# Query projections as whole matmuls up to pair 32, weight loads on SyncE, and two-pair cycles

## The chip, the cores and the metric

The kernel runs on one core of one Trainium2 chip. The metric is device time in microseconds of one execution. TensorE (PE) multiplies into PSUM, VectorE (DVE) and ScalarE (ACT) read PSUM and work on SBUF, GpSimd (POOL) works on SBUF alone, and DMAs are issued from the queues of SyncE (SP), ScalarE and GpSimd. Each engine runs its own instructions in order and waits on semaphores for the others. A transfer that waits at the head of an engine's queue holds up whatever that engine would issue behind it.

## The reference

One transformer block on 2048 tokens of width 512, in float32: attention with 32 query heads of 16 that share one key and one value head, then a gated FFN of inner width 1792.

```python
q = (x @ wq).reshape(B, S, 32, 16)           # per head
k = x @ wk                                   # one head of 16
v = x @ wv
scores = einsum("bhqd,bkd->bhqk", q, k) * 16 ** -0.5
o = einsum("bhqk,bkd->bhqd", softmax(scores), v)
h = A_x + o.reshape(B, S, 512) @ wo          # x above is layernorm(A_x)
y = layernorm(h)
out = h + (gelu(y @ w_gate) * (y @ w_up)) @ w_down
```

Matrix operands are split into a high and a low part, both of type float32r, and a product is the sum of three terms: high by high, high by low, low by high.

## The kernel before

**Tiling.** The 2048 tokens are four blocks of 512 (`NB`, `T`). The 32 heads are eight groups of four (`NG`). Keys come in 16 chunks of 128 (`KC`). A block's attention is thus 8 x 16 key steps, and each key step has two *pairs* of heads. `score(n)` (L1014) issues pair n: two score matmuls into one PSUM tile `s`, one exp on ScalarE (L404) into half of a tile `p`. When a key step's two pairs are done, `weigh` (L406) multiplies `p` by the values into the accumulator `acc`; `finish(k)` (L991) issues the k oldest weighings that are pending. A group is 32 pairs, a block 256.

**Row halves.** A score has a contraction of 50 rows (`KR`): three products of 16 and two rows for a bound that is subtracted before the exp. Keys and queries lie twice in SBUF, at rows 0 and 64. The two score matmuls of a pair take the two row halves of TensorE's array. Where a step of other work is set *beside* a score, the score moves to the one half and the other half takes a matmul with 64 rows of contraction.

**Query projection.** `project_q(b, cs, ...)` (L187) projects block b's queries in four chunks of 128 columns (eight heads). A chunk has 12 terms. As *whole* matmuls with 128 rows they are issued alone, three to a `yield`; as *halves* each term is issued twice, once per half of the rows (lane 0, then lane 1), each beside a score. Between a whole and a half phase, and between lane 0 and lane 1, VectorE copies one column of the bank (`mark`, L211). A finished chunk is split into `qh` and `ql` (two buffers each) and stored to the DRAM tensor `q_d` by three SyncE transfers (L242). For the chunks in `HURRY` VectorE or ScalarE first copies the bank to `raw`, which frees the bank; there is one bank for projections at this point (`width = 1`). After the four chunks the norm of the queries is taken (`pqn`, L255) and the bound row is stored (`bound`, L280) some cycles later, when `age()` says so.

**Order.** Block 0's first chunk is projected in the prologue (`q_first`), and the rest of it (`q_rest`) nearly so: at pair 0 there remain the split of its chunk 3 and its norm. `later_q` (L305) makes the rest: chunk 0 of block 1 whole, chunk 1 half whole and half in halves (`FULL_STEPS`, `BREAK`), all others in halves. `RAMP` gives two steps of it ahead of pairs 3, 5 and 7. From pair 8 to pair 272 (`lead`) the main loop (L1058) runs *cycles* of three pairs: up to four half steps beside the second and third pair, then up to two weighings of key steps that are done, then perhaps one step of weight preparation. Lane 0 takes four halves a cycle; lane 1 takes four or two, by what the cycle before it weighed.

**Weight preparation.** `part_weights` (L495) has 46 steps: it loads 256 KB of wo, w_gate, w_up or w_down, POOL splits it into high and low (and halves w_down), and 512 KB are written to DRAM tensors for the dense part. POOL issues both the load (L503), one step ahead, and the store. Two of three cycles take a step.

**SyncE and VectorE.** Both run an order written out by hand (L1044): what the program issues first stands first in their queues. On SyncE these are the `q_d` stores, `load_q` (L375, issued with the fifth pair of a group for the next group, so 28 pairs ahead), and in block 0 for each finished group the write of the evicted accumulator `oT` to `acc_d` (L425) and its read-back in four transfers to `oc` (L434), which VectorE inverts, multiplies and splits into `o_hi` and `o_lo`.

**End of block 0.** At pair 256 the queries' memory is given back after `check_bound` (L1439), and POOL issues two 1 MB loads of wo. When pair 260 is next, `dense(0)` (L623) is started: two loads of x and four of w1 on SyncE. From pair 272 on the output projection of block 0 (`pp`, L596) runs beside the scores of block 1; its first terms need `o_hi` of chunks 0 to 2, its later ones chunk 3, which is made of groups 6 and 7. The FFN (`pg`, `pu`, `pd`) follows.

Of the kernel before, what the change touches and what calls it, by code (L numbers as in the profile page):

```python
# [9 lines left out]
F32 = mybir.dt.float32  # L10
# [9 lines left out]
P = 128  # L20
# [6 lines left out]
PB = 5  # L27
# [2 lines left out]

W2 = 3

LAG = 6

FIRST_Q = 1

FULL_STEPS = 18

HURRY = ((0, 3), (1, 0))

BREAK = (1, 1)

RAMP = {3: 2, 5: 2, 7: 2}

# [4 lines left out]
CUT, EDGE, GAP, HOLD, REST = -1, -2, -3, -4, -5  # L49
# [3 lines left out]
def kernel(  # L53
# [12 lines left out]
    nc = tc.nc  # L66
# [91 lines left out]
    def run(outer, first):  # L158
# [27 lines left out]

        def project_q(b, cs, eng, col, whole=None):  # L187
            halves = whole is not None
            whole = whole if halves else {c: 3 * DC for c in cs}
            tsl = slice(b * T, (b + 1) * T)  # L190
            xT_hi, xT_lo = xT[b]
            urgent = b == 0 and cs[0] == 0
# [1 line left out]
            for c in cs:  # L194
                pq = psum1(f"pq_{b}_{c}")
                terms = [
                    (wt[:, d, c * P : (c + 1) * P], xt[:, d, :])
                    for d in range(DC)
                    for wt, xt in ((wq_hi, xT_hi), (wq_hi, xT_lo), (wq_lo, xT_hi))
                ]  # L200
                last = len(terms) - 1
                full = whole.get(c, 0)
                for n, (lhsT, rhs) in enumerate(terms[:full]):
                    nc.tensor.matmul(
                        pq, lhsT, rhs, start=(n == 0), stop=(n == last), skip_group_check=full <= last
                    )
                    if n % 3 == 2 and (urgent or n < last):
                        yield 3
                for a in range(2) if full <= last else ():
                    if a or full:  # L210
                        mark = eb.tile([P, 1], F32, tag="qmark", bufs=2, name=f"mark_{b}_{c}_{a}")  # L211
                        nc.vector.tensor_copy(mark, pq[:, :1])
                    rows = slice(64 * a, 64 * a + 64)
                    for n, (lhsT, rhs) in list(enumerate(terms))[full:]:
                        yield a, last - n, partial(
                            nc.tensor.matmul, pq, lhsT[rows], rhs[rows],
                            start=(a == 0 and n == 0), stop=(a == 1 and n == last),
                            skip_group_check=True,
                        )

                raw = None
                if (b, c) in HURRY:
                    raw = eb.tile([P, T], F32, tag="vT", bufs=3, name=f"pq_raw_{b}_{c}")
                    if b == 0:
                        nc.scalar.activation(raw, pq, AF.Copy)
                    else:
                        nc.vector.tensor_copy(raw, pq)
                    yield 3
                qh = eb.tile([P, T], F32R, tag="qh", bufs=2, name=f"qh_{b}_{c}")
                ql = eb.tile([P, T], F32R, tag="ql", bufs=2, name=f"ql_{b}_{c}")  # L230
                if raw is not None:
                    split(nc.vector, qh, ql, raw)
                else:

                    split(nc.vector if b == 0 and c == FIRST_Q else eng, qh, ql, pq)
                qs = eb.tile([P, T], BF16, tag="qs", bufs=DC, name=f"qs_{b}_{c}")
                (nc.gpsimd if urgent else nc.vector).tensor_tensor(
                    qs, qh.bitcast(F32), qh.bitcast(F32), op=ALU.mult
                )
                qss.append(qs)  # L240
                for r0, part in ((0, qh), (DH, ql), (2 * DH, qh)):
                    nc.sync.dma_start(  # L242
                        q_d[c * HC : (c + 1) * HC, r0 : r0 + DH, tsl].bitcast(F32),
                        part.bitcast(F32),
                    )
                if not halves and (raw is None or b == 0):
                    yield 3
                if (b, c) == BREAK:
                    yield HOLD

            if halves:
                yield REST
# [51 lines left out]

        def later_q():  # L305

            second = project_q(1, range(DC), nc.vector, 1, {0: 3 * DC, 1: FULL_STEPS - 3 * DC})
            for _ in range(sum(RAMP.values())):
                yield next(second)

            next(q_rest)
            for token in second:
                if token == HOLD:
                    yield REST
                    for _ in q_rest:
                        pass
                else:
                    yield token
            for b in range(2, NB):
                yield from project_q(b, range(DC), nc.vector, b, {})  # L320

        def age():
            for entry in after:
# [16 lines left out]
        def first_bound(qg):  # L340

            m = ms[0]
            for u in range(2):
                for a, eng in enumerate((nc.sync, nc.scalar)):
                    eng.dma_start(
                        qg[64 * a + 3 * DH : 64 * a + 3 * DH + 1, 2 * u + a, :].bitcast(F32),
                        m[2 * u + a : 2 * u + a + 1, :].bitcast(F32),
                    )
            hs = slice(0, FIRST_Q * HC)
            nc.sync.dma_start(q_d[hs, 3 * DH, :T].bitcast(F32), m[hs].bitcast(F32))  # L350
            for a in range(2):
                nc.sync.dma_start(
                    qg[64 * a : 64 * a + KR, 1 - a :: 2, :].bitcast(F32),
                    q_d.rearrange("h r s -> r h s")[:, 1 - a : 4 : 2, :T].bitcast(F32),
                )

        def advance(gen, n):
            while n > 0:
# [136 lines left out]
        def part_weights(pw):  # L495
# [3 lines left out]


            def load_f(src, name):
                raw = pw.tile([P, D], F32, tag="w_raw", bufs=2, name=f"{name}r")
                nc.gpsimd.dma_start(raw.rearrange("p (c n) -> p c n", n=src.shape[-1]), src)  # L503
                return raw

            def part_f(name, halve, raw):
# [22 lines left out]
            for f in range(FC):  # L529
# [9 lines left out]
                    partial(load_f, wd_t[:, f : f + 1, :], name),  # L539
                    partial(part_f, name, True), partial(store_2, w2_d[f]),  # L540
                ))
            raws, left = {0: steps[0][0]()}, None
            for i, (_, part, store) in enumerate(steps):
                if left is not None:
                    left()
                if i + 1 < len(steps):
                    raws[i + 1] = steps[i + 1][0]()
                both = part(raws.pop(i))
                left = partial(store, both)
                yield 1  # L550
# [440 lines left out]
        def finish(n):  # L991
            for _ in range(min(n, len(pend))):
                pb, pg, pkc, pp, pacc, _ = pend.pop(0)
                weigh(pacc, pp, pkc)
                if pkc == KC - 1:
                    evacuate(pb, pg, pacc)
# [45 lines left out]
        LEAD = (3, 2, 2)  # L1042
        n, lead = 0, 2 * PER + sum(SIZES[: LEAD[0]])
        with tc.manual_schedule(engines={mybir.EngineType.SP, mybir.EngineType.DVE}):  # L1044
            parts, said = None, 3
            if first:
                work = later_q()
                parts = part_weights(early.enter_context(tc.tile_pool(name="parts", bufs=1)))

            while n < 2 * PB - 2:  # L1050
                for _ in range(RAMP.get(n, 0) if first else 0):
                    next(work)
                score(n)
                n += 1
            finish(len(pend) - 2)

            token, ran = next(work) if first else None, 2
            for cycle in range((lead - n) // 3):  # L1058
                age()
                rest = token == REST  # L1060
                count = 0
                if token is not None and not rest:
                    count = min(4 if ran < 2 or token[0] == 0 else 2, token[1] + 1)
                for j in range(3):
                    if n == 2 * PER:
                        assert token is None
                        while after:
                            age()
                        for _ in parts or ():
                            pass  # L1070
                        if first:
                            check_bound(eb, k2m)
                        parts = work = None
                        early.close()
                        db = late.enter_context(tc.tile_pool(name="dense", bufs=1))
                        load_wo(0)
                    if 0 < j <= count // 2:
# [15 lines left out]
                finish(ran)  # L1093
                if outs:
                    take_out()
                if parts is not None and cycle > 2 and cycle % 3 < 2:
                    next(parts, None)
            assert n == lead
        assert not outs
# [421 lines left out]
```

## Time and profile before

| | |
|---|---|
| Time, median of 3 runs | 1446.84 us (1445.14 to 1448.3) |
| Profiled execution, time | 1445.67 us |
| Profiled execution, span | 1444.0 us |
| TensorE busy | 1406.6 us (97%) |
| ScalarE busy | 1041.9 us (72%) |
| VectorE busy | 542.3 us (38%) |
| GpSimd busy | 231.3 us (16%) |
| Mean granted TensorE clock | 0.992 |
| Exps (L404) | 1024, 1029 ns each |
| Moved by DMA | 194.09 MB, 134 GB/s on average |

The span runs from the first to the last instruction, and the device time has a little around it. A busy TensorE isn't TensorE at its peak: matmuls are pipelined, and each shows as busy from its start to its modelled end, so overlapping ones hide how closely they follow one another. A row of the timeline gives the start, the time that it covers, the engine and the line, what is written from what, and how many instructions were merged; in brackets stands the idle time ahead of it and what ended that.

### The profile page before, as it was taken

Reading aid. Unit: us, or ns where it says so; the run is one execution under the profiler, and the core shown is the slowest. Engines: PE = TensorE matmul, PEld = TensorE weight load, DVE = VectorE, ACT = ScalarE, POOL = GpSimd, SP = SyncE. Lnnn points to the kernel's source line nnn. Section 1 sums busy time; section 2 is a strip of 40 time slices with the busy share of each in tenths; the row PEclk is TensorE's granted clock in tenths of the full one; section 3 lists DMA queues with packets and bytes.
Section 4 is the critical chain, followed back from the end, with each engine's and each line's share of the span. In section 5 each row is a group of like instructions: output and inputs, shape, how many; then the busy total and the mean of one; then the engine's idle time right before and its main releaser. Section 6 shows DMA issues by size and latency. Waiting matters only on the chain.

```text
span 1444.0 us, 25562 instructions
## 1 busy us (share of the span) xinstructions
PE 1406.6 (97%) x10628; PEld 789.6 (55%) x10628; DVE 542.3 (38%) x975; ACT 1041.9 (72%) x1149; POOL 231.3 (16%) x332
## 2 busy tenths in 40 slices
PE   9799999997999999999999999999999999999998
PEld 7433333333555555555555555555565555557886
DVE  7411313211344332423344242423344242426665
ACT  7489999996777777787777777777777787773000
POOL 6447677650100000000000000000000000002000
PEclk9899999998999999999999999999999999999999
DMA  4556776754144141305144231324144231435551
GB/s 156 157 172 235 240 234 219 222 183 158 41 172 143 41 146 53 132 27 202 51 149 143 70 135 36 132 85 143 56 143 143 83 124 36 144 125 202 176 203 63
DMA packets 71224, 194.09 MB, mean 134 GB/s; under 512 B 9696, under 2 KB 9696, under 8 KB 71068
## 3 DMA queue, kind: packets, MB, share of 16 engines
q1 hardware_dynamic: 60052, 154.00, 31.5%
q0 software_dynamic: 10880, 38.28, 8.0%
q8 instruction: 85, 1.39, 0.4%
q14 instruction: 39, 0.32, 0.1%
q10 hardware_dynamic: 168, 0.10, 0.0%
HBM read 142.53 MB, written 49.55 MB: 133 GB/s over the span
## 4 chain that ended last, share of the span: by engine, by line
PE 86%; ACT 6%; DMA 3%; DVE 2%; issue 1%; SPq 1%; POOL 0%; ACTq 0%; DVEq 0%; POOLq 0%
PE acc L408 30%; PE s L400 18%; PE pu L919 10%; PE pg L919 7%; ACT p L404 6%; PE pd L919 4%; PE pd L596 3%; PE pd L618 3%; PE pg L618 3%; PE pu L618 3%; PE pq L398 2%; PE pp L596 2%; DMA acc_d<-oT 1%; PE pp L727 1%; DMA q_d<-qh 1%
## 5 line engine op out<-in xcount | busy, mean ns | idle before, releaser
L404 ACT ACTIVATE p<-s 128x1024 f32<-128x1024 f32 x1024 | 970.5, 1029 | 259.6 <-PE s L400 257.8
L408 PE MATMUL acc<-p,v_sb 128*32 128x512 f32 x4096 | 493.6, 601 | 0.2 <-DVE oT L421 0.2
L400 PE MATMUL s<-qg,kaug 50*128 50x512 f32 x1984 | 422.1, 427 | 8.9 <-ACT p L404 8.7
L400 PEld LDWEIGHTS s<-qg,kaug 50*128 50x128 f32 x1984 | 191.0, 184 | 259.4 <-ACT p L404 131.4
L408 PEld LDWEIGHTS acc<-p,v_sb 128*32 128x32 f32 x4096 | 112.5, 109 | 237.8 <-issue 233.4
L919 PE MATMUL pu<-x2h,w 64*128 64x512 f32 x672 | 211.5, 391 | 0.0
L919 PE MATMUL pg<-x2h,w 64*128 64x512 f32 x672 | 211.0, 390 | 0.0
L919 PEld LDWEIGHTS pu<-x2h,w 64*128 64x128 f32 x672 | 115.8, 185 | 16.8
L919 PEld LDWEIGHTS pg<-x2h,w 64*128 64x128 f32 x672 | 116.0, 185 | 11.5 <-DVE h L861 0.2
L919 PE MATMUL pg<-x2l,w 64*128 64x512 f32 x336 | 121.9, 390 | 0.0
L919 PE MATMUL pu<-x2l,w 64*128 64x512 f32 x336 | 121.8, 390 | 0.0
L129 POOL TENSOR_SCALAR rstd<-mv 128x1 f32<-128x1 f32 x16 | 3.5, 222 | 683.9 <-DVE mv L127 683.8
L796 ACT ACTIVATE ga<-ga 128x512 f32<-128x512 f32 x56 | 35.3, 634 | 89.2 <-DVE ga L791 89.2
L919 PE MATMUL pd<-w,gh 64*128 64x512 f32 x384 | 81.2, 392 | 0.0
L861 DVE TENSOR_TENSOR h<-h,pd 128x512 f32<-128x512 f32 x48 | 31.9, 684 | 115.5 <-PE pd L919 66.4
L448 DVE RECIPROCAL oc<-oc 128x128 f32<-128x128 f32 x64 | 56.4, 921 | 38.2 <-DMA oc<-acc_d 33.5
L1148 DVE SCALAR_TENSOR_TENSOR ga<-ga,g 128x512 f32<-128x512 f32 x70 | 48.3, 691 | 52.2 <-ACT ga L796 51.1
L919 PEld LDWEIGHTS pu<-x2l,w 64*128 64x128 f32 x336 | 57.9, 185 | 8.1
L780 DVE COPY g<-pg 128x512 f32<-128x512 f32 x56 | 38.7, 692 | 62.5 <-PE pg L919 56.8
L919 PEld LDWEIGHTS pg<-x2l,w 64*128 64x128 f32 x336 | 58.0, 185 | 6.0
L421 DVE COPY oT<-acc 128x512 f32<-128x512 f32 x32 | 22.1, 691 | 89.3 <-PE acc L408 89.1
L793 DVE TENSOR_TENSOR g<-g,pu 128x512 f32<-128x512 f32 x56 | 38.2, 682 | 40.2 <-PE pu L919 30.3
(277 smaller groups left out, 1487.3 us busy)
## 6 DMA issues: line engine op xcount, KB each, us to landing
w<-w_d SPq DMA_DIRECT2D x112, 512.0 KB
w<-w_d SPq DMA_DIRECT2D x28, 1024.0 KB
qg<-q_d SPq DMA_DIRECT2D x48, 200.0 KB
q_d<-qh SPq DMA_DIRECT2D x32, 256.0 KB
acc_d<-oT SPq DMA_DIRECT2D x31, 256.0 KB
oc<-acc_d SPq DMA_DIRECT2D x124, 64.0 KB
w_d<-w_0b POOLq DMA_DIRECT2D x14, 512.0 KB, 5.0
w_d<-w_1b POOLq DMA_DIRECT2D x14, 512.0 KB, 5.7
```

Of the source, the lines that this page charges most:

```text
L400: nc.tensor.matmul(s[:, a, :], kaug[rows, kc * P : (kc + 1) * P], qg[rows, 2 * u + a, :], start=True, stop=True,)
L404: nc.scalar.activation(p[:, 2 * u : 2 * u + 2, :], s, AF.Exp, scale=SCALE)
L408: nc.tensor.matmul(acc[32 * j : 32 * j + 32, :], v_sb[:, kc, :], p[:, j, :], start=(kc == 0), stop=(kc == KC - 1), skip_group_check=True,)
L448: nc.vector.reciprocal(oc[:, 1, sl], oc[:, 1, sl])
L596: nc.tensor.matmul(banks[k], lhsT[rows], rhs[rows], start=(turn == 0 and i == 0), stop=(turn == 1 and i == n - 1), skip_group_check=True,)
L618: nc.tensor.matmul(bank, lhsT, rhs, start=(i == 0), stop=(i == len(ts) - 1))
L780: nc.vector.tensor_copy(g, pg)
L793: nc.vector.tensor_tensor(g, g, pu, op=ALU.mult)
L796: nc.scalar.activation(a, a, AF.Tanh, scale=GELU_A * GELU_C)
L861: nc.vector.tensor_tensor(hs[t], hs[t], pd, op=ALU.add)
L919: nc.tensor.matmul(e["bank"], lhsT[rows], rhs[rows], start=i == 0 and not e["both"], stop=last and e["both"], skip_group_check=True,)
L1148: (soon or lazy).pop(0)()
```

## The change

`RAMP` stays, but up to pair 32 (`2 * KC`) there are only whole matmuls: chunks 0 and 1 of block 1 are both whole, and chunk 1 joins `HURRY`, so its bank is copied out at once. After the ramp one step of `later_q` is taken ahead of every fourth pair (11, 15, 19, ...) until it yields 0, which it does behind block 0's norm. Every fourth pair, all but two pending weighings are issued, and at pairs 16, 20, 28 and 32 one step of weight preparation. `first_bound` no longer loads the second copy of group 0's queries, which only pairs with a step beside them need.

From pair 32 on the cycles run as before, with three differences. After every third finished chunk, lane 1 of the next one takes four halves in each cycle. Weight preparation is stepped by the pair number (`n % 9 != 8`). And once projection has ended, a cycle that begins at an even pair has two pairs in place of three.

The weight loads are issued on SyncE, three steps ahead, into four buffers in place of two. POOL keeps the splits and the stores.

```diff
+AHEAD_W = 3
-FULL_STEPS = 18
-HURRY = ((0, 3), (1, 0))
-BREAK = (1, 1)
+HURRY = ((0, 3), (1, 0), (1, 1))
...
-                for a in range(2) if full <= last else ():
-                    if a or full:
+                for a in range(2) if not full else ():
+                    if a:
...
-            second = project_q(1, range(DC), nc.vector, 1, {0: 3 * DC, 1: FULL_STEPS - 3 * DC})
+            second = project_q(1, range(DC), nc.vector, 1, (0, 1))
             for _ in range(sum(RAMP.values())):
                 yield next(second)
             next(q_rest)
-            for token in second:
-                if token == HOLD:
-                    yield REST
-                    for _ in q_rest:
-                        pass
-                else:
-                    yield token
+            for _ in range(2 * DC - sum(RAMP.values())):
+                yield next(second)
+            yield from q_rest
+            yield 0
+            yield from second
...
             hs = slice(0, FIRST_Q * HC)
             nc.sync.dma_start(q_d[hs, 3 * DH, :T].bitcast(F32), m[hs].bitcast(F32))
-            for a in range(2):
-                nc.sync.dma_start(
-                    qg[64 * a : 64 * a + KR, 1 - a :: 2, :].bitcast(F32),
-                    q_d.rearrange("h r s -> r h s")[:, 1 - a : 4 : 2, :T].bitcast(F32),
-                )
...
-                raw = pw.tile([P, D], F32, tag="w_raw", bufs=2, name=f"{name}r")
-                nc.gpsimd.dma_start(raw.rearrange("p (c n) -> p c n", n=src.shape[-1]), src)
+                raw = pw.tile([P, D], F32, tag="w_raw", bufs=AHEAD_W + 1, name=f"{name}r")
+                nc.sync.dma_start(raw.rearrange("p (c n) -> p c n", n=src.shape[-1]), src)
...
-            raws, left = {0: steps[0][0]()}, None
+            raws, left = {i: steps[i][0]() for i in range(AHEAD_W)}, None
             for i, (_, part, store) in enumerate(steps):
                 if left is not None:
                     left()
-                if i + 1 < len(steps):
-                    raws[i + 1] = steps[i + 1][0]()
+                if i + AHEAD_W < len(steps):
+                    raws[i + AHEAD_W] = steps[i + AHEAD_W][0]()
...
-            parts, said = None, 3
+            parts, said = None, 3 if first else 0
...
-            while n < 2 * PB - 2:
-                for _ in range(RAMP.get(n, 0) if first else 0):
-                    next(work)
+            while n < 2 * KC:
+                for _ in range(RAMP.get(n, n > 7 and n % 4 == 3) if said else 0):
+                    said = next(work)
+                    age()
                 score(n)
                 n += 1
-            finish(len(pend) - 2)
+                if n % 4 == 0:
+                    finish(len(pend) - 2)
+                    if parts is not None and n > 12 and n % 24:
+                        next(parts)
-            token, ran = next(work) if first else None, 2
-            for cycle in range((lead - n) // 3):
+            token, ran, done = next(work) if first else None, 2, 0
+            while n < lead:
...
-                    count = min(4 if ran < 2 or token[0] == 0 else 2, token[1] + 1)
-                for j in range(3):
+                    count = min(4 if ran < 2 or token[0] == 0 or done % 3 == 0 else 2, token[1] + 1)
+                    done += token[0] == 1 and token[1] + 1 == count
+                for j in range(2 if token is None and n % 2 == 0 else 3):
...
-                if parts is not None and cycle > 2 and cycle % 3 < 2:
+                if parts is not None and n % 9 != 8:
                     next(parts, None)
```

More of the change, by code (lines that the diff above doesn't have):

```diff
@@ L188, in project_q @@
             halves = whole is not None
-            whole = whole if halves else {c: 3 * DC for c in cs}
+            whole = whole if halves else cs
             tsl = slice(b * T, (b + 1) * T)
@@ L201, in project_q @@
                 last = len(terms) - 1
[L202 to L205, printed above, removed]
-                    )
+                full = c in whole
+                for n, (lhsT, rhs) in enumerate(terms if full else ()):
+                    nc.tensor.matmul(pq, lhsT, rhs, start=(n == 0), stop=(n == last))
                     if n % 3 == 2 and (urgent or n < last):
                         yield 3
-                for a in range(2) if full <= last else ():
-                    if a or full:
-                        mark = eb.tile([P, 1], F32, tag="qmark", bufs=2, name=f"mark_{b}_{c}_{a}")
+                for a in range(2) if not full else ():
+                    if a:
+                        mark = eb.tile([P, 1], F32, tag="qmark", bufs=2, name=f"mark_{b}_{c}")
                         nc.vector.tensor_copy(mark, pq[:, :1])
                     rows = slice(64 * a, 64 * a + 64)
-                    for n, (lhsT, rhs) in list(enumerate(terms))[full:]:
+                    for n, (lhsT, rhs) in enumerate(terms):
                         yield a, last - n, partial(
@@ L247, in project_q @@
                     yield 3
-                if (b, c) == BREAK:
-                    yield HOLD
             if halves:
@@ L311, in later_q @@
             next(q_rest)
-            for token in second:
-                if token == HOLD:
-                    yield REST
-                    for _ in q_rest:
-                        pass
-                else:
-                    yield token
+            for _ in range(2 * DC - sum(RAMP.values())):
[3 more added lines that the diff above has]
+            yield from second
             for b in range(2, NB):
-                yield from project_q(b, range(DC), nc.vector, b, {})
+                yield from project_q(b, range(DC), nc.vector, b, ())
         def age():
@@ L350, in first_bound @@
             nc.sync.dma_start(q_d[hs, 3 * DH, :T].bitcast(F32), m[hs].bitcast(F32))
-            for a in range(2):
-                nc.sync.dma_start(
-                    qg[64 * a : 64 * a + KR, 1 - a :: 2, :].bitcast(F32),
-                    q_d.rearrange("h r s -> r h s")[:, 1 - a : 4 : 2, :T].bitcast(F32),
-                )
         def advance(gen, n):
```

## The prediction

> **What bounds the kernel now.** I read the 40 slices first, for where an engine falls away, then ScalarE's instructions in order of time, then what stood ahead of each gap, and last the same stretch of a later block for comparison.
>
> ```profile
> span 1444.0 us, 25562 instructions
> ...
> ACT  7489999996777777787777777777777787773000
> ```
>
> ScalarE is at 9 from slice 4 on, which is the attention of block 0 with the query projections beside it; from slice 10 the FFN shares TensorE and ScalarE is no bound. The change touches slices 1 to 10, so I went through the exps there. One exp (L404) is one pair.
>
> ```profile
> 61.28 1.02 ACT L404 ACTIVATE p<-s 128x1024 f32<-128x1024 f32 x1 [1.29 <-PE s L400]
> 70.66 1.94 ACT L404 ACTIVATE p<-s 128x1024 f32<-128x1024 f32 x2 [8.36 <-PE s L400]
> ...
> 96.67 5.61 ACT L404 ACTIVATE p<-s 128x1024 f32<-128x1024 f32 x6 [0.45 <-PE s L400]
> 102.70 5.61 ACT L404 ACTIVATE p<-s 128x1024 f32<-128x1024 f32 x6 [0.42 <-PE s L400]
> ...
> 320.39 16.89 ACT L404 ACTIVATE p<-s 128x1024 f32<-128x1024 f32 x18 [0.19 <-PE s L400]
> 337.48 1.94 ACT L404 ACTIVATE p<-s 128x1024 f32<-128x1024 f32 x2 [0.20 <-PE s L400]
> 340.10 1.94 ACT L404 ACTIVATE p<-s 128x1024 f32<-128x1024 f32 x2 [0.68 <-PE s L400]
> 351.06 1.94 ACT L404 ACTIVATE p<-s 128x1024 f32<-128x1024 f32 x2 [9.02 <-PE s L400]
> ```
>
> Stretches of the same trace (columns: PE, PEld, DVE, ACT, POOL busy with their counts, clock, DMA share, GB/s):
>
> ```profile
> 51.69:96.67 44.98, 36.40 (x233) 15.18 (x231) 9.24 (x16) 30.28 (x32) 15.86 (x22) 0.89 0.54 178
> 96.67:308.79 212.12, 208.12 (x1504) 80.19 (x1500) 50.60 (x75) 196.30 (x210) 154.37 (x187) 1.00 0.73 230
> 308.79:337.48 28.69, 26.00 (x182) 8.06 (x178) 1.44 (x4) 27.98 (x30) 6.87 (x11) 1.00 0.59 213
> 338.08:384.85 46.77, 37.95 (x278) 19.62 (x279) 19.02 (x34) 25.33 (x28) 4.01 (x9) 0.89 0.17 55
> 668.65:703.38 34.73, 34.10 (x271) 18.11 (x270) 13.74 (x27) 25.95 (x28) 3.51 (x8) 1.00 0.36 133
> ```
>
> By their ACT counts (32, 210, 30) pair 32 starts at 96.67, pair 242 at 308.79, pair 272 at 337.48. Three rates follow. ScalarE with nothing to wait for: (5.61 - 1.02) / 5 = 0.918 us a pair (six in a row, one alone). With row halves beside: 6 pairs in 102.70 - 96.67 = 6.03, so 1.005, and 212.12 / 210 = 1.010 over the whole stretch with its small bumps. With three-pair cycles and no projection: (337.48 - 320.39) / 18 = 0.949. The two large gaps are 8.36 us ahead of pair 9 and 9.02 us ahead of pair 276, and the granted clock is 0.89 in the two stretches that hold them and 1.00 elsewhere.
>
> The first gap:
>
> ```profile
> 55.94 10.46 DMA q_d<-qh
> 66.52 0.43 DVE L119 CAST qh<-pq_raw 128x512 fp32r<-128x512 f32 x1 [3.95 <-DMA q_d<-qh]
> 68.53 0.68 DVE L237 TENSOR_TENSOR qs<-qh 128x512 bf16<-128x512 f32 x1
> 69.14 0.14 DVE L212 COPY mark<-pq 128x1 f32<-128x1 f32 x1
> 69.33 0.79 PE L398 MATMUL pq<-xT_hi,wq_hi 64*128 64x512 f32 x1 [8.12 <-DVE mark L212]
> 71.41 3.64 PE L408 MATMUL acc<-p,v_sb 128*32 128x512 f32 x16
> ```
>
> A store of q_d takes 10.46 us; the split of chunk 3 of block 0 waits for its buffer; the one-column mark that joins whole and half terms stands behind that split on VectorE; TensorE's first half waits for the mark, and scores stand behind it. TensorE then returns at a reduced clock, so that sixteen acc matmuls take 3.64 us. The second:
>
> ```profile
> 323.97 1.38 SPq L630 DMA_DIRECT2D xb<-in_A_x_dram  x2
> 324.86 0.69 DVE L421 COPY oT<-acc 128x512 f32<-128x512 f32 x1 [4.50 <-PE acc L408]
> 325.40 2.60 SPq L556 DMA_DIRECT2D w<-w_d  x4
> 328.05 12.99 DMA acc_d<-oT
> 341.06 1.73 SPq L434 DMA_DIRECT2D oc<-acc_d  x4
> 344.68 3.39 DVE L448 RECIPROCAL oc<-oc 128x128 f32<-128x128 f32 x4 [19.13 <-DMA oc<-acc_d]
> 349.31 1.22 PE L596 MATMUL pp<-wo,o_hi 64*128 64x512 f32 x4 [8.37 <-DVE o_hi L459]
> ```
>
> The last heads of block 0 are out of PSUM at 325.55, but dense(0) put six loads, 2.5 MB by their tile shapes, into SyncE's queue first; the 256 KB write lands after them, and the output projection waits for what comes out of it.
>
> **The change part by part.** Order of issue I derived by counting through both versions of the loop.
>
> *Pairs 0 to 31.* Chunk 1 of block 1 becomes whole: 6 whole matmuls in place of 12 halves and two marks. No half and no mark is issued before pair 32, so the wait at 69.33 has nothing left to stand on. To pair 8 the order is that of before (61.28 stays). After it come one step of three matmuls at pairs 11 and 15, the norm of block 0 at 19, and two weighings at every fourth pair.
>
> ```profile
> 53.58 0.73 PE L400 MATMUL s<-qg_first,kaug 50*128 50x512 f32 x4
> 54.24 0.50 PE L204 MATMUL pq<-xT_hi,wq_hi 128*128 128x512 f32 x1
> 55.83 0.73 PE L400 MATMUL s<-qg_first,kaug 50*128 50x512 f32 x4
> ...
> 58.86 1.92 PE L408 MATMUL acc<-p,v_sb 128*32 128x512 f32 x16
> 60.72 0.49 PE L400 MATMUL s<-qg_first,kaug 50*128 50x512 f32 x2
> ```
>
> Two pairs of scores take 54.24 - 53.58 = 0.66, two weighings 60.72 - 58.86 = 1.86. Two steps, six matmuls, take 55.83 - 54.24 = 1.59; one of three I estimate at 0.85, half of it and a little for the turn. Four pairs: 1.32 + 1.86 + 0.85 = 4.03 on TensorE, against 4 x 0.918 = 3.67 on ScalarE, and without a step 3.18. So the steps show a little and the rest is ScalarE's. Bounds for the 24 pairs from 61.28: 22.0 (all at 0.918) and 25.8 (4.3 for each four, a weighing's bubble added everywhere); I take 24.0, since two weighings in a row left 0.42 a time in the rows of six. Pair 32 then starts at 85.3, **11.4 us** earlier (9.6 to 13.4).
>
> The removed second halves of qg_first are two SyncE transfers ahead of the q_d stores: no one waits for them before pair 32, and by then each group's own load carries both halves. I price this at nothing, with a gain inside the next rival's margin.
>
> *Pairs 32 to 238.* The same two rates of halves; in every third chunk the second lane takes four a cycle in place of two. In the rows of six, cycles of the first lane, which always take four, cost the same 6.03 as those of the second, so I price it at 0 (up to 2 us lost if a second-lane cycle is not like the first; 0.5 gained). Projection ends at pair 239 where it ended at 242.
>
> *Pairs 239 to 271.* Before: 3 x 1.010 + 28.69 = 31.7. After, two scores and one weighing a cycle, 0.66 + 0.93 = 1.6 of TensorE under 1.84 of ScalarE: at 0.918 to 0.949, 30.3 to 31.3; I take 30.7, **1.0 us** gained.
>
> *The end of block 0.* With two-pair cycles the last weighing falls behind pair 257, not 259, so the eviction and its write are issued ahead of pair 260's dense(0): write and read-back stand in SyncE's queue before the six loads. What such a write takes beside the weight traffic:
>
> ```profile
> 197.13 1.25 SPq L425 DMA_DIRECT2D acc_d<-oT  x1
> 205.13 1.71 SPq L434 DMA_DIRECT2D oc<-acc_d  x4
> ...
> 260.18 0.36 SPq L425 DMA_DIRECT2D acc_d<-oT  x1
> 263.41 1.72 SPq L434 DMA_DIRECT2D oc<-acc_d  x4
> ```
>
> SyncE issues the read when the write has landed: 3.2 us at best, 8.0 at worst. On the clock of the old trace: eviction done near 324.2, landed at 327.4 to 332.2, read back 3.6 later (341.06 to 344.68), VectorE 4.6 (344.68 to 349.31), so o_hi at 335.6 to 340.4. The terms that need it come near 340.7. The stall goes; its worth is the whole stretch against the same one of block 1: 46.77 - 34.73 = **12.0 us** (0 if o_hi is as late as now). What is late next: the six loads go out some 5 us later, but their first user, pg, stands 35 us behind pp.
>
> *Weights from SyncE.* 46 loads leave POOL,
>
> ```profile
> L503 POOL DMA_DIRECT2D w_1r<-in_B_w_up_dram x14 | 10.8, 772 | 1.3 <-issue 1.3
> ```
>
> where the issue of one takes it up to 0.77 us, and stand in SyncE's queue, each behind the release of its buffer by part i-1. Behind a held load stand q_d stores, the acc_d writes and the next group's qg. A qg load is issued 4 pairs into a group and needed 28 pairs later; that is the cover, about 28 us less a landing of 4. The loop asks for 45 more steps in the 205 pairs from pair 16 on, 4.6 us each. POOL is busy 154.37 of 212.12 us now, issues included; 46 x 0.77 = 35 us of load issues go, so the same work in 207 us keeps it at 0.6, and a load has three steps, 13.8 us, to land. I price the move at 0; without the cover a qg is late by what SyncE is held beyond 24 us (rival 3).
>
> By the Trainium skill (DMA: Bandwidth & Descriptors, Queues, rings and completion order) descriptors of one issuing row are consumed in ring order and rows take turns; so weight loads on SyncE's row would stand ahead of an acc_d write there, where on POOL's row they only alternated with it. Three loads, 0.77 MB at 230 GB/s, would make 3.3 us, as an estimate; at the end of block 0 no weight load is left, so the sum by that rule is the same, and only the rival on SyncE gains by it.
>
> **Sum.** 11.4 + 0 + 1.0 + 12.0 = 24.4. Profiled execution 1445.67 (span 1444.0 and 1.67 around it): 1421.3. It lies 1.2 under the median shown, 0.08%, and I leave it there: **1421**.
>
> **Rivals.**
> 1. *The write at the end of block 0 is still late*: it now goes out together with the two 1 MB loads of wo on POOL's queue. For: the 12.99 us. Against: 4.75 MB were in flight then, 2.25 now, and check_bound is reached earlier, with POOL no longer behind. Decides from a landing of 8.3 us on; with all 12.0 lost, 1433.
> 2. *The first gap moves to the norm at pair 19*, which needs chunk 1 copied out; that copy is behind the same split, which waits for the same store. By the old times VectorE is through at 69.2 + 0.7 = 69.9 and TensorE is there near 72.3. A store 5 us slower costs 2.6, the whole wait 8.4: 1430. Against it: two loads fewer before that store.
> 3. *SyncE becomes the line that all stand in (slower).* A load is held until POOL has finished part i-1; POOL goes slowly where its data are late:
>
> ```profile
> 143.74 0.62 POOL L119 CAST w_0b<-w_0r 128x512 fp32r<-128x512 f32 x1
> ...
> 161.96 0.61 POOL L119 CAST w_0b<-w_0r 128x512 fp32r<-128x512 f32 x1 [1.26 <-DMA w_0r<-in_B_w_gate_dram]
> ```
>
> Three parts in 18.2, 6.07 each. At that pace throughout, 45 x (6.07 - 4.6) = 66 us behind; less the cover of 24, 42 on the path: 1463. It decides against the change from 5.7 us a part (45 x 1.1 = 49, less 24). Against: those gaps were for a load issued one part ahead; three ahead cover 13.8 us.
>
> **How the numbers follow.** Forecast 0.72, rival 1 0.12, rival 2 0.09, rival 3 0.07. The bounds of the costed terms alone give 1419 to 1425; the range takes in rivals 1 and 2: 1416 to 1433. Under 0.2%, about 3 us, nothing can be told from no change here. Forecast and rivals 1 and 2 hold 0.93, rival 3 0.07; one hundredth of each side is left for a time that cannot be told from before: faster 0.92, same 0.02, slower 0.06.
>
> **What would show it.** Right: no wait over 2 us ahead of an exp between pairs 8 and 272; pair 32 near 85 us, pair 272 near 325; granted clock 1.0 in both old dips; acc_d's write of group 7 ahead of xb in SyncE's order and landed within 8 us; pp to pg in 35 us. Wrong: a gap at pair 19, SyncE waiting on POOL for more than some microseconds, a qg landing late, or a gap at pp again. The forecast falls if two of the three gains are absent.

## The result, and the profile after

The changed kernel takes 1424.17 us (median of 4 runs, 1424.0 to 1424.85), the kernel before on the same chip 1445.99 (4 runs, 1444.88 to 1448.3). The ratio is 0.9848, with a 95% interval of 0.9831 to 0.9865: 21.8 us less, where 1421 was forecast. The profiled execution took 1424.32 us and spans 1422.6.

ScalarE's exps in order of time, changed kernel (pairs 8, 12, 28, 32, 242 and 274 begin these rows):

```profile
61.34 3.77 ACT L391 ACTIVATE p<-s 128x1024 f32<-128x1024 f32 x4 [1.29 <-PE s L387]
65.45 3.77 ACT L391 ACTIVATE p<-s 128x1024 f32<-128x1024 f32 x4 [0.34 <-PE s L387]
...
81.45 3.77 ACT L391 ACTIVATE p<-s 128x1024 f32<-128x1024 f32 x4 [0.19 <-PE s L387]
85.44 2.85 ACT L391 ACTIVATE p<-s 128x1024 f32<-128x1024 f32 x3 [0.21 <-PE s L387]
...
297.16 29.44 ACT L391 ACTIVATE p<-s 128x1024 f32<-128x1024 f32 x32 [0.19 <-PE s L387]
327.56 3.77 ACT L391 ACTIVATE p<-s 128x1024 f32<-128x1024 f32 x4 [0.96 <-PE s L387]
```

And its stretches (the columns are those of the prediction; the last runs from the first pp to the first pg):

```profile
51.73:85.44 33.71, 31.28 (x207) 12.59 (x205) 7.80 (x13) 30.30 (x33) 12.76 (x17) 1.00 0.60 200
85.44:297.16 211.72, 209.41 (x1522) 82.05 (x1518) 49.98 (x80) 196.29 (x210) 133.73 (x154) 1.00 0.74 242
297.16:324.66 27.50, 27.18 (x180) 8.41 (x178) 5.89 (x8) 27.50 (x31) 1.51 (x2) 1.00 0.54 184
325.57:361.56 35.99, 35.39 (x279) 19.14 (x280) 13.83 (x27) 24.94 (x28) 4.02 (x9) 1.00 0.18 57
```

Both large gaps are gone, and the clock is 1.00 in all four stretches. Pair 32 starts at 85.44 (96.67 before), pair 242 at 297.16 (308.79), pair 272 at 297.16 + 30 x 0.917 = 324.66 (337.48), where 0.917 is (29.44 - 1.02) / 31. From pp to pg it is 35.99 us against 46.77.

The end of block 0, changed kernel, rows of SyncE, POOL, VectorE and TensorE in order of time:

```profile
296.90 0.36 SPq L1435 DMA_DIRECT2D b_d<-q2m  x1
302.66 1.52 POOL L557 DMA_DIRECT2D wo<-wo_d  x2 [6.81 <-PE s L387]
...
311.98 0.34 SPq L412 DMA_DIRECT2D acc_d<-oT  x1
314.04 1.72 SPq L421 DMA_DIRECT2D oc<-acc_d  x4
316.25 0.82 SPq L617 DMA_DIRECT2D xb<-in_A_x_dram  x2
...
322.05 0.43 DVE L446 CAST o_hi<-oc 128x512 fp32r<-128x512 f32 x1
325.57 0.73 PE L583 MATMUL pp<-wo,o_hi 64*128 64x512 f32 x4 [0.24 <-issue]
```

The write of group 7 stands ahead of dense(0)'s loads and lands in 2.1 us; `o_hi` is there 3.1 us before the first pp. The first two rows show what the prediction named only in passing, in the argument against its rival 1, and put no time on: `check_bound`'s store, behind which the queries' memory is given back, goes out at 296.90, 13 us ahead of pair 256 (309.99). In the kernel before it went out at 320.59, 2 us ahead of that pair:

```profile
317.20 0.63 POOL L520 DMA_DIRECT2D w_d<-w213b  x1 [0.30 <-POOL w213b L120]
319.58 0.53 DVE L281 TENSOR_SCALAR m<-qn,mm 32x512 fp32r<-32x512 f32 x1 [11.61 <-POOL mm L274]
320.59 0.36 SPq L1443 DMA_DIRECT2D b_d<-q2m  x1
```

POOL stores its last weight part at 317.20 and only then comes to the factors of block 3's bound. VectorE waits 11.61 us for them, writes the bound row `m`, and `check_bound`'s store follows 1.0 us behind. The same 1.0 us lies between `m` and that store in the changed kernel (295.88 and 296.90), so in both kernels the release waits for the last bound row.

The gain shrinks a little on the way to the end. One eviction early in block 1, and the one that is last but one, first in the kernel before and then in the changed one:

```profile
370.49 0.69 DVE L421 COPY oT<-acc 128x512 f32<-128x512 f32 x1 [1.33 <-PE acc L408]
1262.38 0.69 DVE L421 COPY oT<-acc 128x512 f32<-128x512 f32 x1 [3.98 <-PE acc L408]
```

```profile
347.19 0.69 DVE L408 COPY oT<-acc 128x512 f32<-128x512 f32 x1 [1.33 <-PE acc L395]
1241.08 0.69 DVE L408 COPY oT<-acc 128x512 f32<-128x512 f32 x1 [3.99 <-PE acc L395]
```

23.3 us are won by the first and 21.3 are left at the second. The two were lost in steps of about half a microsecond in a part that the change does not touch; no run was made for them.

### The profile page after: what moved, and what is told of

Read it like the earlier page. It is cut to its first block, busy times and chain, and to the rows that moved or that the text cites. A ratio compares the mean times of both kernels' runs of the same rounds, so it can differ in the third digit from the quotient of the medians.

```text
span 1422.6 us, 25583 instructions
## 1 busy us (share of the span) xinstructions
PE 1402.0 (99%) x10622; PEld 788.0 (55%) x10622; DVE 539.4 (38%) x974; ACT 1041.9 (73%) x1149; POOL 202.4 (14%) x286
## 4 chain that ended last, share of the span: by engine, by line
PE 88%; ACT 7%; DVE 1%; issue 1%; DMA 1%; POOL 0%; SPq 0%; ACTq 0%; DVEq 0%; POOLq 0%
PE acc L395 31%; PE s L387 19%; PE pu L906 8%; PE pg L906 8%; ACT p L391 7%; PE pd L906 5%; PE pd L583 3%; PE pd L605 3%; PE pg L605 3%; PE pu L605 3%; PE pq L385 2%; PE pp L583 2%; PE pq L202 1%; PE pp L714 1%; PE pxt L650 1%
```

## The experiments

The first three kernels undo one part of the change each, the next three make one part each in the kernel before, and two more vary one number of the changed kernel. All times are medians; each stands beside the ratio to the kernel before, run on the same chip, whose medians in the three sets were 1445.22, 1444.69 and 1445.57. The runs of the kernel before spread from 1438 to 1452 us there, those of the changed kernel from 1424.0 to 1424.85 on its own chip. Where a time is set against the changed kernel's 1424.17, it is a median from another chip; by the ratios such a difference comes out 1.5 to 4 us larger, and each ratio has an interval of 2.4 to 5.2 us to each side. So the argument rests on the gaps in the profiles first, and each profile is of one execution.

**Cycles of three to the end.**

```diff
-                for j in range(2 if token is None and n % 2 == 0 else 3):
+                for j in range(3):
```

> The changed kernel with cycles of three pairs to the end of the lead, all else as changed. Theory of the prediction (the order of issue frees the write of group 7): the eviction falls behind pair 260 again, its write stands behind the six loads of dense(0), pp waits as before: 10 to 12 us lost and 1 us of pace in the last 33 pairs, 1435 to 1437. Rival (POOL, no longer behind, lets the queries' memory go early, so SyncE issues the six loads ahead of time and they are through before the eviction): only the pace is lost, 1425 to 1427, and acc_d's write lands in under 6 us though it stands behind the loads in the queue.

Measured 1424.54 us (1423.57 to 1425.9), ratio 0.9873 (0.9855 to 0.9891): no loss that can be told, since this interval and that of the changed kernel (0.9831 to 0.9865) overlap. SyncE in that kernel:

```profile
300.22 1.80 SPq L617 DMA_DIRECT2D xb<-in_A_x_dram  x2
302.06 2.64 SPq L543 DMA_DIRECT2D w<-w_d  x4
313.92 0.32 SPq L412 DMA_DIRECT2D acc_d<-oT  x1
316.56 1.73 SPq L421 DMA_DIRECT2D oc<-acc_d  x4
```

The write stands behind the six loads, as in the kernel before, and yet lands in 2.6 us: the loads went out 12 to 14 us ahead of it, since the memory was free by then (`check_bound`'s store went out at 296.88). The rival held. Here it doesn't matter that the loads are first in the queue, because the memory is free so long before the eviction. In every kernel here whose loads stand ahead of the write they go out 3.3 to 3.9 us behind `check_bound`'s store.

**Loads back on POOL, one step ahead, two buffers.**

```diff
-                raw = pw.tile([P, D], F32, tag="w_raw", bufs=AHEAD_W + 1, name=f"{name}r")
-                nc.sync.dma_start(raw.rearrange("p (c n) -> p c n", n=src.shape[-1]), src)
+                raw = pw.tile([P, D], F32, tag="w_raw", bufs=2, name=f"{name}r")
+                nc.gpsimd.dma_start(raw.rearrange("p (c n) -> p c n", n=src.shape[-1]), src)
...
-            raws, left = {i: steps[i][0]() for i in range(AHEAD_W)}, None
+            raws, left = {0: steps[0][0]()}, None
...
```

> The changed kernel with the weight loads back on POOL, one step ahead and into two buffers. Theory of the prediction (the move is priced at 0): 1423 to 1426. Rival: POOL keeps its old pace of 5.2 us a part and is done near 317, while pair 256 is now reached near 310; the bound's factors wait behind the parts on POOL, the bound's store and check_bound behind them on SyncE, and with them the eviction's write and the loads of wo: o_hi and wo come 5 to 10 us late, 1429 to 1434, with pp waiting near 326.

Measured 1427.87 (1427.2 to 1429.36), ratio 0.9895 (0.9878 to 0.9913): 3.7 us over the changed kernel's median. Neither expectation had the place right. The rival had its time 1 us off and its gap in the wrong spot: nothing waits at pp, and POOL is through with the parts at 298.7. The gap is in the middle, ahead of pair 177. VectorE there:

```profile
231.23 0.53 DVE L275 TENSOR_SCALAR m<-qn,mm 32x512 fp32r<-32x512 f32 x1 [11.82 <-POOL mm L268]
231.69 0.67 DVE L117 CAST qh<-pq 128x512 fp32r<-128x512 f32 x1
232.40 0.69 DVE L118 TENSOR_TENSOR ql<-pq,qh 128x512 fp32r<-128x512 f32 x1
```

POOL and TensorE there:

```profile
228.19 1.28 POOL L118 TENSOR_TENSOR w_0b<-w_0r,w_0b 128x512 fp32r<-128x512 f32 x1
229.57 0.26 POOL L259 TENSOR_SCALAR mm<-q,k2m 32x1 f32<-32x1 f32 x1
...
233.14 0.79 PE L385 MATMUL pq<-xT_hi,wq_hi 64*128 64x512 f32 x1 [2.19 <-DVE ql L118]
```

`bound` needs POOL's four small operations on `mm`, and these stand in POOL's queue behind weight parts that are late. VectorE waits 11.82 us; the next chunk's split stands behind `bound`; the one projection bank is not free until that split is done; and TensorE, with scores behind the projection's next half, stands still for 2.2 us. The price is more than twice that: pair 242 starts at 302.01, 4.9 us later than in the changed kernel, since the granted clock is 0.69 between 231 and 242 us, where the changed kernel has 1.00. The changed kernel has this wait too, 7.81 us on VectorE, but not long enough to stop TensorE.

**The first 32 pairs as before**, with loads on SyncE and two-pair cycles (later_q, project_q, first_bound and the first loop are the lines with a minus in the diff of the change).

> The changed kernel with the first 32 pairs as before (halves from pair 8 on, chunk 1 half whole, one mark between, both copies of group 0's queries loaded), weights on SyncE and two-pair cycles kept. Prediction: the 8.4 us wait behind the mark and the slow clock after it come back, pair 32 near 96 to 97, 11 us lost: 1434 to 1437. Rival (the wait came from weight loads that shared the DMA engines with the q_d stores; these now start later): the wait is under 4 us, 1427 to 1431.

Measured 1427.44 (1427.08 to 1428.23), ratio 0.9892 (0.9875 to 0.9908): 3.3 us, not 11. Exps of this kernel:

```profile
61.28 1.02 ACT L406 ACTIVATE p<-s 128x1024 f32<-128x1024 f32 x1 [1.28 <-PE s L402]
67.28 1.94 ACT L406 ACTIVATE p<-s 128x1024 f32<-128x1024 f32 x2 [4.97 <-PE s L402]
71.28 2.85 ACT L406 ACTIVATE p<-s 128x1024 f32<-128x1024 f32 x3 [2.07 <-PE s L402]
```

Its chain of waits has, where the kernel before has 10.46 us for the store:

```profile
56.16 7.79 DMA q_d<-qh
```

The gap behind the mark is there, but 4.97 us long. The store lands 2.7 us sooner. What differs ahead of it is that POOL issued the first two weight loads at 54.09 and 54.88 us in the kernel before, while SyncE comes to them at 80.26 here. The gap is 4.97 and 4.68 us in the two kernels with such late loads (this one and the next), and 8.22 to 8.41 in the three with loads on POOL and the mark (the kernel before and two below). The 11 us that I had foretold did not come; the rival's time was right, though its wait was to be under 4. Pair 32 is at 92.2, 6.8 us later than in the changed kernel, pair 272 at 329.8, 5.1 later: halves begun at pair 8 are done sooner, and the cheaper pairs without projection begin sooner.

**Only the loads moved to SyncE**, in the kernel before.

> The kernel before with only the weight loads moved to SyncE, three ahead, four buffers. Theory of the prediction: no change, 1444 to 1447. Rival of u_three (POOL on time frees memory early, so the six loads are through before the eviction of group 7): the gap ahead of pair 276 shrinks from 9 us to under 3 us, 1434 to 1438. Second rival (loads held at SyncE's head hold up the q_d stores): a longer first gap, 1448 or more.

Measured 1435.03 (1429.98 to 1443.44 in ten runs), ratio 0.9927 (0.9901 to 0.9952): 10.2 us gained by the part that I had priced at nothing; the time is in the first rival's range, and the runs lie 13 us apart; the profile is of one that took 1438.62. In it both large gaps shrink: the first to 4.68 us, and the one at pair 276 is gone. `check_bound`'s store goes out at 314.14, 6.5 us earlier than in the kernel before, and the loads at 317.47, ahead of the write at 328.96. A new gap comes, 4.55 us at pair 224, the first of group 7, where a qg is late; TensorE's waits for a qg between 80 and 340 us (us in all, how often, the longest):

```profile
PE s L402 <- DMA qg<-q_d: 3.3, 2, 2.6
```

**Only the two-pair cycles**, in the kernel before.

> The kernel before with only the two-pair cycles once projection has ended. Theory of the prediction: the eviction is issued ahead of dense(0)'s loads, the gap ahead of pair 276 goes and 1 us of pace is gained: 1433 to 1436. Rival (POOL is behind until 317 and holds the bound's store, which stands ahead of the write on SyncE): the write goes out at most 3 us earlier than before and shares the engines with wo; half of the gap stays, 1439 to 1442.

Measured 1439.55 (1433.44 to 1442.38 in ten runs), ratio 0.9959 (0.994 to 0.9978). In its profile the gap at pair 276 is gone, as the prediction's order has it, though `check_bound`'s store is as late as in the kernel before:

```profile
321.15 0.36 SPq L1445 DMA_DIRECT2D b_d<-q2m  x1
328.97 0.34 SPq L425 DMA_DIRECT2D acc_d<-oT  x1
...
336.88 0.84 SPq L630 DMA_DIRECT2D xb<-in_A_x_dram  x2
```

A gap of 4.24 us stands at pair 177, behind `bound`, in which VectorE waits 14.66 us for POOL. The time is in the rival's range, but not for the rival's reason: none of the gap at pair 276 stays, and the loss is elsewhere.

**Only the first 32 pairs**, in the kernel before, with lane 1's pace.

> The kernel before with only its first 32 pairs as changed (whole chunks 0 and 1, no mark, steps ahead of every fourth pair) and the pace of lane 1 that goes with it, so that projection ends in time; weight loads on POOL, cycles of three pairs. Prediction: 11 us gained at pair 32 and kept: 1434 to 1436. Rival (POOL cannot keep up when the pairs go faster: its parts end near 317 whatever the pairs do): the 11 us are spent again at the end of block 0, where check_bound and the release of memory wait for POOL: 1440 to 1446.

Measured 1435.57 (1433.91 to 1437.18), ratio 0.9941 (0.9921 to 0.9962): 9.1 us. Pair 32 starts at 85.46, as in the changed kernel, so the term of 11.2 us is reproduced. Then comes a gap of 8.80 us at pair 177 behind `bound`, and with it and the slow clock after it nearly all is lost again: pair 242 starts at 307.87, 0.9 us earlier than in the kernel before. What the run has gained in the end comes from pair 276, where there is no gap, though the loads of dense(0) stand ahead of the write: they began to go out 13 us before it. So the time is where I had put it, but by luck: the 11 us were not kept. The rival was right that POOL spends what the pairs gain, and wrong about the place.

**Four halves in every cycle of lane 1.**

```diff
-                    count = min(4 if ran < 2 or token[0] == 0 or done % 3 == 0 else 2, token[1] + 1)
+                    count = min(4, token[1] + 1)
```

> The changed kernel with four halves in every cycle of lane 1, not only in every third chunk. By the count of cycles projection then ends some 18 pairs earlier, which run at 0.92 in place of 1.005 a pair. Theory (a second-lane cycle with four halves costs what one with two costs): 1.5 us gained, 1422 to 1423.5. Rival (the extra halves make those cycles longer): 1425 or more.

Measured 1425.38 (1422.56 to 1428.85), ratio 0.9883 (0.9847 to 0.9919): inconclusive, the runs lie 6 us apart. In the profile pair 272 starts at 323.56, 1.1 us earlier than in the changed kernel, but that profile is of the fastest of the four.

**Loads on SyncE one step ahead.**

```diff
-AHEAD_W = 3
+AHEAD_W = 1
```

> The changed kernel with the weight loads on SyncE only one step ahead, into two buffers. If the three steps are what covers the landing of a load and the release of its buffer: POOL waits for each load, SyncE is held by POOL for longer, some parts come late and the end of block 0 waits: 1426 to 1432. Rival (taking the issue off POOL is enough): 1424 to 1425.

Measured 1452.35 (1448.85 to 1453.94), ratio 1.0053 (1.003 to 1.0077): slower than the kernel before, and 28 us slower than with three steps. Both expectations missed this. Two waits of the trace, of VectorE and TensorE, between 80 and 330 us (us in all, how often, the longest):

```profile
DVE m L275 <- POOL mm L268: 40.3, 2, 21.0
...
PE pq L385 <- DVE ql L118: 23.2, 2, 11.6
```

The gaps of 11.26 and 11.77 us, at pairs 96 and 177, are both `bound` waiting for POOL, and POOL waits up to 15 us for a load.

The last four put the bound of blocks 1 to 3 later, so that VectorE meets POOL's factors 14 cycles after the norm:

```diff
-            after.extend([[2, factors], [4, bound]])
+            after.extend([[2, factors], [4 if b == 0 else 14, bound]])
```

> ahead1 (changed kernel, loads one step ahead) with the bound of blocks 1 to 3 issued 14 cycles after the norm, not 4, so that VectorE has two more splits behind it before it meets a late POOL. Theory (POOL is behind with its parts, VectorE waits in bound for POOL's factors, the next chunk's split waits behind it, TensorE's one bank waits for the split): the gaps of 11 to 12 us that stand behind VectorE's m go, about 25 us: 1425 to 1433. Rival (late loads hold SyncE, and q_d or qg are late): the gaps stay under another releaser, 1445 or more.

Measured 1451.69 (1449.04 to 1453.85), ratio 1.0052 (1.0034 to 1.0071): nothing gained. My theory had foretold 1425 to 1433. What TensorE waited for, of the same kind as above:

```profile
PE s L387 <- DMA qg<-q_d: 14.2, 5, 4.3
PE pqn L249 <- DVE ql L118: 4.8, 1, 4.8
...
PE pq L385 <- DVE ql L118: 1.1, 1, 1.1
```

The wait behind `bound` fell from 23.2 to 1.1 us, so that half of the theory holds, and its price came back in another place: gaps of 5.08, 4.11 and 6.95 us now stand at pairs 128, 192 and 224, where a group begins and its qg is late, and one of 7.90 at pair 158, in which the norm of block 2 waits for VectorE. SyncE in this kernel, a wait and an issue:

```profile
SPq L490 <- POOL w_1b L118: 19.0, 7, 3.9
```

```profile
292.23 2.94 SPq L367 DMA_DIRECT2D qg<-q_d  x2
```

This qg is group 7's. The program issues it with pair 196, which starts near 270.4; SyncE comes to it 22 us later, about half of it since weight loads ahead of it are held by POOL's buffers (10.5 us of waits for POOL there); 5.6 us of it are a wait for an accumulator's write. With one step ahead both lines are late together, and taking one away only shows the other.

> u_pool (changed kernel, loads on POOL, one ahead) with the bound 14 cycles after the norm. Theory: what moving the loads to SyncE is worth is this wait alone; without it 1424 to 1425.5, and no gap near pair 177. Rival (the loads' issue on POOL costs elsewhere too): stays at 1427 to 1428.

Measured 1423.54 (1423.16 to 1423.6), ratio 0.9861 (0.9828 to 0.9894). No gap over 1.1 us between pairs 9 and 272, and pair 242 starts at 297.19, where the changed kernel has 297.16. With the bound out of the way no difference can be told by who issues the loads.

> The kernel before with the bound 14 cycles after the norm, nothing else. Its own profile shows VectorE waiting up to 11.6 us for POOL without a gap on ScalarE; the large gaps at pairs 9 and 276 have other causes. Theory: the two large gaps stay, only the spread from run to run shrinks: 1440 to 1445. Rival (the late bound is behind the gap at pair 276 as well): 1434 to 1438.

Measured 1445.43 (1443.3 to 1449.82), ratio 1.0005 (0.9987 to 1.0024): no difference. The two large gaps stay (8.41 us at pair 9, 11.33 at pair 276). So the waits behind the bounds of blocks 1 and 2 are behind neither. Of block 3's bound the run can't say this: later or not, it is made when POOL is through with the parts, and `check_bound` stands behind it (`m` at 323.14, the store at 324.18). The spread stayed over 6 us, so the spread of the kernel before is not explained by it alone.

> lane4 (changed kernel, four halves in every cycle of lane 1) with the bound 14 cycles after the norm. lane4 gained 1.1 us at pair 272 in its profile and its runs spread over 6 us. Theory (the spread is the wait for POOL): 1422 to 1424, spread under 2 us. Rival: the spread stays.

Measured 1423.08 (1422.51 to 1423.74), ratio 0.9859 (0.9826 to 0.9892). The spread is 1.2 us where lane4 had 6.3. Against the changed kernel's ratio of 0.9848 no difference can be told; neither it nor u_pool_late is shown to be faster.

## Why the prediction was right, step by step

**First gap (11.4 us forecast).** Pair 32 came 96.67 - 85.44 = 11.2 us earlier, and the way there was as forecast: with a step 4.1 us for four pairs (61.34 to 65.45), without 3.99 (81.45 to 85.44), against 4.03 and 3.67; the mark and the wait behind it are gone. What the step left out is that the loads' later start alone takes a part of it: the store's 10.46 us were made longer by weight loads, and u_early loses 6.8 us at pair 32, not 11.2, and 3.3 at the end.

**Pairs 32 to 271 (0 and 1.0).** 211.72 us for 210 pairs against 212.12, then 27.50 for 30 against 28.69: 1.6 us together. The two-pair cycles' pace is 1.2 of these at pair 272 (325.8 in u_three against 324.66), but u_three ends within 0.4 us of the changed kernel, so even that is not kept.

**End of block 0 (12.0).** pp to pg became shorter by 46.77 - 35.99 = 10.8 us. The result is right and the order of issue is what was derived, but the reason given was one of two that each suffice, so that the term came out is in part luck. *The eviction and its write are issued ahead of pair 260's dense(0)* removes the gap where memory comes free late (a_two). Where it comes free early, the loads are through before the eviction, and the order does not matter (u_three, a_sp, a_early). It comes free late when POOL is late with the factors of the last bound (320.59 in the kernel before). In the changed kernel both reasons hold, and taking the two-pair cycles away costs nothing that can be told.

**Weights from SyncE (0).** This is the step that failed: *I price the move at 0*. Alone it gains 10.2 us, taken back it costs 3.7. The term was priced by what might wait behind a held load on SyncE, not by who waits behind a late POOL. In the changed kernel these are `bound` on VectorE, the next split, the one bank and TensorE, and u_pool_late shows that this wait is the whole worth of the move there: without it the loads can stay on POOL. In the profile of the kernel before, the bounds of blocks 1 and 2 make no gap; there the move gains by other ways, as a_sp's profile has them: the first gap is 3.7 us shorter, since the loads start later, and POOL is on time with the last bound's factors, so the memory comes free early and the gap at pair 276 goes. The longest time from the issue of an accumulator's write to that of its read, for groups 0 to 6, grew from 8.0 to 9.05 us with the loads in the same queue,

```profile
154.93 1.41 SPq L412 DMA_DIRECT2D acc_d<-oT  x1
163.98 1.73 SPq L421 DMA_DIRECT2D oc<-acc_d  x4
```

1.1 us, where the Trainium skill's rule of ring order (DMA: Bandwidth & Descriptors, Queues, rings and completion order) had been turned into an estimate of 3.3; it cost the changed kernel nothing.

**Rivals.** Rivals 1 and 2 did not come. Rival 3 names a real mechanism at its real place, SyncE held by POOL and qg late. It is a gap of 4.55 us in a_sp. In ahead1, 28 us over the changed kernel, it stands together with the wait for `bound`, and ahead1_late shows it without that wait. Three steps ahead are what keeps the changed kernel from it, so the 13.8 us of cover in the prediction were the right argument; its price of 42 us was for another pace.

**Sum.** 11.2 + 1.6 + 10.8 = 23.6 against 24.4, less the 2 us that went later: 21.4 of span, 1444.0 to 1422.6. The time was inside the range. That the parts add up here does not make them additive. Taken away singly they cost 3.3, 0.4 and 3.7, which makes 7.3 (by the ratios 6.4, 3.6 and 6.8, which makes 16.8). Alone they gain 9.1, 5.1 and 10.2, and that this makes 24.4 is chance: in all three the stretch from pp to pg falls to 35.9 or 36.0 us, so the 10.8 us of the end of block 0 are counted three times, and the waits at pairs 177 and 224 take about as much away.

## What to carry to other kernels

A stall with two sufficient remedies is not explained by the one that was applied: undo each part singly and also make each singly, and look where the two sums differ. When work is moved between queues, list for every engine what waits *for* the queue that is relieved, not only what stands behind the moved work in its new queue; a helper of four small operations behind a lagging producer stopped TensorE here, by way of VectorE and the one bank. And a stall can cost more than it lasts: 2.2 us of it made the pairs behind 4.9 us late. When a wait is taken away and the time stays, look for a second line that was late by as much.

## What the runs showed of the hardware

The issue of the same load of w_gate takes POOL 0.77 us (the row of 772 ns for w_up in the prediction is its twin), and SyncE 0.37 where it did not wait:

```profile
75.77 0.37 SPq L490 DMA_DIRECT2D w_0r<-in_B_w_gate_dram  x1
```

A gap of TensorE of 8.1 us was followed by sixteen acc matmuls in 3.64 us in the kernel before (1.92 at the full clock). In u_early, behind a gap of 4.74 us, such a set took 2.79:

```profile
65.95 0.79 PE L400 MATMUL pq<-xT_hi,wq_hi 64*128 64x512 f32 x1 [4.74 <-DVE mark L214]
...
68.03 2.79 PE L410 MATMUL acc<-p,v_sb 128*32 128x512 f32 x16
```

How long the clock stays low does not follow from the length of the gap alone. By the granted clock in stretches of a microsecond or half of one, TensorE runs at 0.50 for some 5.7 us after its return in the kernel before, for 3.9 in u_early, but for 6.5 in u_pool, behind a gap of only 2.19 us, and in a_sp a gap of 2.35 us is followed by none. What sets it stays open here.
